# The last chunk of a fused Fourier mixing and feed-forward kernel: product order, sums read from PSUM, three queues for its stores

## The chip, the core and the metric

The kernel runs on one NeuronCore of a Trainium2 chip. A core has five engines with instruction streams of their own: TensorE (PE, matrix products), VectorE (DVE, elementwise), ScalarE (ACT, one-input functions and copies with a scale), GpSimd (POOL, elementwise in software) and SyncE (SP, which mainly issues transfers). They meet at semaphores. Transfers between on-chip memory (SBUF) and device memory are issued from the queues of SP, ACT or POOL and are carried out by the core's DMA engines. Products land in PSUM, from which ACT and DVE can read.

The metric is the device time of one execution in microseconds (us), lower is better.

## The reference

```python
def _attn_ref(x):                       # x: (8, 3008, 256), float32
    X = np.fft.fft(x, axis=1)
    X = np.fft.fft(X, axis=2)
    return X.real.astype(np.float32)

def _moe_ref(x, w_in, w_out):           # x: the result above as (24064, 256)
    h = x @ w_in                        # w_in: (256, 2048)
    relu6 = np.clip(h + 3.0, 0.0, 6.0)
    g = h * relu6 / 6.0
    return (g @ w_out).astype(np.float32)   # w_out: (2048, 256)
```

The real part of a two-dimensional Fourier transform of each of 8 sequences, then a feed-forward layer with the hard-swish function.

## The kernel before

The sequence axis of 3008 = 47 × 64 is transformed in two stages of matrix products (`stage1`, `stage2`). The transform along the 256 features is folded into the first weight matrix. The 8 sequences are worked in 4 pairs. Each pair's frequencies are cut into chunks of up to 256 columns, and a chunk holds frequencies together with their mirror images, so that one pass through `w_in` serves both: `mlp1` makes two products u and v, and u + v and u − v are the hidden values of a frequency and of its mirror.

A chunk takes 8 steps (`fc` = 0 to 7), each of which handles two blocks of 128 hidden units. The order of the work is written out by hand: a loop over all steps of all chunks calls `mlp1` two steps ahead, `combine` one step ahead, and `mlp2` for the step itself, with the transform stages of the next pair and the finishing of the previous chunk put between at fixed steps.

The second product (`mlp2`) uses a scheme of Strassen's kind: seven products of 128x128 weight blocks in place of eight. Their moving operands are three of the activated blocks, `a`, and four sums of them, `c`, which `combine` makes in three additions, one after another (the last of them is the operand of product 6). The seven products accumulate over the 8 steps in four PSUM tiles, `ch.acc[0]` to `ch.acc[3]`: products 0 and 1 in the first, 2 and 3 in the second, 4 and 5 in the third, 6 in the fourth. Product 3's operand is the first of the `c`.

At a chunk's last step ACT copies the tiles to an SBUF tile `e`, scaled by 1 / WS (line 472). The four output blocks are then sums of products: with P0 to P6 for the scaled products, in `r[m, h]`, where `m` is the frequency or its mirror and `h` a half of the features,

- r[0, 0] = P0 + P1
- r[0, 1] = P0 − P5 + P3 + P6
- r[1, 0] = P0 − P5 + P4 + P2
- r[1, 1] = P0 − P5 + P4 + P3

For all chunks but the last, `finish` makes these on GpSimd in the background. Each block is then turned in 32x32 squares by VectorE (`turn`, line 522) into a tile `o`, and each `o` leaves in stores of 32 KB (`send`, line 528), each with 4 x 32 runs of 256 B.

For the very last chunk (`ch.final`, 192 columns) nothing is left to hide behind, and it has a path of its own. `combine` of its last step runs on VectorE. ACT evacuates only the first two PSUM tiles. `finish_final` makes the sums on VectorE, reading products 4 to 6 straight from PSUM through `add_product` (line 498), turns each block as soon as it is made, and sends the first `o` (m = 0, 6 stores) before it makes the second (m = 1, 6 stores). The stores alternate between the queues of SP and ACT.

After the last instruction come the closing waits and a barrier of all engines, which the profile books under the line of the program's launch, L1001 before the change and L1008 after it. Every engine goes through a DRAIN there before the barrier. SP waits for the semaphores of all transfers.

Of the kernel before, what the change touches and what calls it, by code (L numbers as in the profile page):

```python
# [48 lines left out]
WS = 2.0 ** 20  # L49
# [9 lines left out]
def kernel(  # L59
# [10 lines left out]
    nc = tc.nc  # L70
# [4 lines left out]
    NF = NFC // 2  # L75
# [35 lines left out]
    out_k = out.rearrange("(p bj i k1) (q e) -> p k1 bj q i e", p=NP, k1=N1, i=DH, e=2 * DH)  # L111
# [325 lines left out]
    def add(out, in0, in1, eng=None):  # L437
        (eng or nc.gpsimd).tensor_tensor(out, in0, in1, op=AL.add)  # L438
# [17 lines left out]
    def mlp2(ch, fc):  # L456
        a = ch.a.pop(fc)[:].rearrange("p m f n -> p (m f) n")[:, :, 0:ch.n]
        c = ch.c.pop(fc)
        moving = [a[:, 0], a[:, 1], a[:, 3], c[:, 0], c[:, 1], c[:, 2], c[:, 3]]
        for i, mv in enumerate(moving):  # L460

            if fc == 0 and i % 2 == 0:
                ch.acc[i // 2] = ps_a.tile([P, 2, TB], F32, tag="acc", name="acc")
            nc.tensor.matmul(ch.acc[i // 2][:, i % 2, 0:ch.n], G[:, i, fc, :], mv,  # L464
                             start=(fc == 0 and i % 2 == 0), stop=(fc == NF - 1), skip_group_check=True)
            if fc == NF - 1 and (i % 2 == 1 or i == 6):
                if i == 1:
                    ch.e = epool.tile([P, 8, TB], F32, tag="e", name="e")
                k = 2 * (i // 2)
                if ch.final and k >= 4:  # L470
                    continue
                nc.scalar.mul(ch.e[:, k:i + 1, 0:ch.n], ch.acc[i // 2][:, 0:i + 1 - k, 0:ch.n], 1.0 / WS)  # L472

# [14 lines left out]

    def finish_final(ch):
        n = ch.n  # L490
        e = ch.e[:, :, 0:n]
        w = epool.tile([P, 3, TB], F32, tag="w", bufs=1, name="w")
        ch.r = epool.tile([P, 2, 2, TB], F32, tag="r", name="r")
        wn, rn = w[:, :, 0:n], ch.r[:, :, :, 0:n]
        os = [epool.tile([P, TB // DH, 2, DH], F32, tag="o", name="o") for m in range(2)]

        def add_product(out, i, in1, sign=1.0):
            nc.vector.scalar_tensor_tensor(out, ch.acc[i // 2][:, i % 2, 0:n], sign / WS, in1,
                                           op0=AL.mult, op1=AL.add)

        add(rn[:, 0, 0], e[:, 0], e[:, 1], nc.vector)
        turn(ch, os[0], 0, 0)
        add_product(wn[:, 0], 5, e[:, 0], -1.0)
        add(wn[:, 2], wn[:, 0], e[:, 3], nc.vector)
        add_product(rn[:, 0, 1], 6, wn[:, 2])
        turn(ch, os[0], 0, 1)
        send(ch, os[0], 0)
        add_product(wn[:, 1], 4, wn[:, 0])
        for h in range(2):
            add(rn[:, 1, h], wn[:, 1], e[:, 2 + h], nc.vector)  # L510
            turn(ch, os[1], 1, h)
        send(ch, os[1], 1)

    def store(ch, m):
        o = epool.tile([P, TB // DH, 2, DH], F32, tag="o", name="o")
        for h in range(2):
            turn(ch, o, m, h)
        send(ch, o, m)

    def turn(ch, o, m, h):  # L520
        n = ch.n
        nc.vector.transpose(o[:, 0:n // DH, h], ch.r[:, m, h, 0:n].rearrange("p (j i) -> p j i", i=DH))  # L522

    def send(ch, o, m):

        queues = [nc.sync, nc.scalar] if ch.final else [nc.sync]
        for j, (bj, k1) in enumerate(ch.blocks[m]):
            queues[j % len(queues)].dma_start(out=out_k[ch.pr.p, k1, bj], in_=o[:, j].rearrange("p h e -> p (h e)"))

    pairs = [Pair(p) for p in range(NP)]  # L530
    first = pairs[0]
# [347 lines left out]
    for s, (p, ck, fc) in enumerate(steps):  # L879
# [24 lines left out]
        else:  # L904
# [8 lines left out]
            if prev and fc < 3:  # L913
                if fc > 0:
                    store(prev, fc - 1)
                elif not prev.first:
                    finish(prev)
            mlp2(*chunk(s))
        if fc == NF - 1:
            prev = chunks[p][ck]  # L920
    finish_final(prev)


# [82 lines left out]
```

## Time and profile before

| | |
|---|---|
| median of 3 runs | 1947.92 us (1947.09 to 1950.45) |
| span of the profiled execution | 1945.0 us |
| TensorE matmul busy | 1927.7 us, 99% of the span |
| VectorE / GpSimd / ScalarE busy | 1437.7 / 1416.1 / 682.5 us |
| granted TensorE clock, mean | 0.998 |
| DMA, mean over the span | 50 GB/s |

The page gives the busy time of each engine, the chain of waits that ended last, the groups of instructions by line, and the transfers. The chain is TensorE's for 94% of the span. The change, however, concerns only what comes at the very end. There the last product begins at 1935.10 us, the last instruction of VectorE at 1938.16 us, and the span ends at 1945.03 us. The queries that matter are therefore the timeline and the table of stretches for the last 15 us, and the instructions of the closing block. The busy time of an engine says nothing here, since from 1935.4 us on no engine has much to do.

### The profile page before, as it was taken

Reading aid. Unit: us, or ns where it says so; the run is one execution under the profiler, and the core shown is the slowest. Engines: PE = TensorE matmul, PEld = TensorE weight load, DVE = VectorE, ACT = ScalarE, POOL = GpSimd, SP = SyncE. Lnnn points to the kernel's source line nnn. Section 1 sums busy time; section 2 is a strip of 40 time slices with the busy share of each in tenths; the row PEclk is TensorE's granted clock in tenths of the full one; section 3 lists DMA queues with packets and bytes.
Section 4 is the critical chain, followed back from the end, with each engine's and each line's share of the span. In section 5 each row is a group of like instructions: output and inputs, shape, how many; then the busy total and the mean of one; then the engine's idle time right before and its main releaser. Section 6 shows DMA issues by size and latency. Waiting matters only on the chain.

```text
span 1945.0 us, 27925 instructions
## 1 busy us (share of the span) xinstructions
PE 1927.7 (99%) x9254; PEld 1658.3 (85%) x9254; DVE 1437.7 (74%) x2777; ACT 682.5 (35%) x1167; POOL 1416.1 (73%) x1620
## 2 busy tenths in 40 slices
PE   9999999999999999999999999999999999999997
PEld 4678888888998888888898888888899888888887
DVE  6877777777777777777787777777778777777777
ACT  5633333333333333333333333333333333333332
POOL 4078888877688887787678887878666667666664
PEclk9999999999999999999999999999999999999999
DMA  8531312211112132111111221212110101101000
GB/s 235 170 80 40 81 48 57 55 44 31 39 28 55 49 81 57 44 50 31 38 36 45 57 55 44 49 52 52 35 28 20 28 17 27 35 12 28 20 19 20
DMA packets 148959, 96.71 MB, mean 50 GB/s; under 512 B 117791, under 2 KB 131235, under 8 KB 148814
## 3 DMA queue, kind: packets, MB, share of 16 engines
q1 hardware_dynamic: 137350, 58.06, 12.5%
q0 software_dynamic: 10672, 36.67, 6.7%
q8 instruction: 73, 1.20, 0.3%
q14 instruction: 72, 0.59, 0.1%
q10 hardware_dynamic: 792, 0.20, 0.0%
HBM read 57.57 MB, written 37.32 MB: 49 GB/s over the span
## 4 chain that ended last, share of the span: by engine, by line
PE 94%; DVE 3%; ACT 1%; DMA 1%; issue 0%; SPq 0%; DVEq 0%; POOL 0%; ACTq 0%
PE acc L464 56%; PE v L379 16%; PE u L379 16%; PE ps L328 2%; PE ps L223 1%; DVE a L424 1%; PE acc L448 1%; DMA xt<-in_x_dram,IX 1%; DVE s L384 1%; ACT t L421 1%; PE spare L635 0%; DVE o L522 0%; DVE u L405 0%; ACT PM L574 0%; PE ps L278 0%
## 5 line engine op out<-in xcount | busy, mean ns | idle before, releaser
L438 POOL TENSOR_TENSOR c<-a 128x512 f32<-128x512 f32 (+1 forms) x375 | 469.5, 1252 | 363.5 <-PE acc L464 317.5
L464 PE MATMUL acc<-c,G 128*128 128x256 f32 (+1 forms) x3008 | 696.9, 374 | 0.0
L421 ACT ACTIVATE t<-u,half 128x512 f32<-128x512 f32 (+1 forms) x384 | 260.7, 679 | 1143.7 <-DVE u L394 1064.7
L464 PEld LDWEIGHTS acc<-c,G 128*128 128x128 f32 x3008 | 565.4, 190 | 71.1
L384 DVE SCALAR_TENSOR_TENSOR s<-qn,WN,u 128x256 f32<-128x256 f32 (+1 forms) x768 | 330.1, 471 | 333.4 <-PE u L379 332.6
L464 PE MATMUL acc<-a,G 128*128 128x256 f32 (+1 forms) x2256 | 541.2, 375 | 0.0
L464 PEld LDWEIGHTS acc<-a,G 128*128 128x128 f32 x2256 | 421.3, 189 | 71.2 <-issue 17.5
L379 PE MATMUL v<-q,W 127*128 127x256 f32 (+1 forms) x1536 | 389.0, 375 | 2.3 <-DVE a L424 2.3
L379 PE MATMUL u<-q,W 128*128 128x256 f32 (+1 forms) x1536 | 388.0, 375 | 0.0
L424 DVE SCALAR_TENSOR_TENSOR a<-t,u 128x512 f32<-128x512 f32 (+2 forms) x448 | 263.7, 600 | 103.4 <-ACT t L421 99.6
L379 PEld LDWEIGHTS v<-q,W 127*128 127x128 f32 x1536 | 288.3, 190 | 42.1 <-DVE a L424 1.9
L379 PEld LDWEIGHTS u<-q,W 128*128 128x128 f32 x1536 | 285.7, 190 | 35.2 <-issue 0.5
L438 POOL TENSOR_TENSOR c<-a,c 128x256 f32<-128x256 f32 (+1 forms) x375 | 269.0, 717 | 29.4
L438 POOL TENSOR_TENSOR c<-c,a 128x256 f32<-128x256 f32 (+1 forms) x375 | 268.8, 717 | 29.4
L394 DVE TENSOR_TENSOR u<-s,v 128x512 f32<-128x512 f32 x352 | 245.0, 696 | 38.1 <-DVE s L384 1.8
L424 DVE SCALAR_TENSOR_TENSOR a<-t,v 128x512 f32<-128x512 f32 (+1 forms) x480 | 263.4, 565 | 0.2
L421 ACT ACTIVATE t<-v,half 128x512 f32<-128x512 f32 (+1 forms) x384 | 260.6, 679 | 0.5 <-PE acc L464 0.4
L396 DVE TENSOR_TENSOR v<-v,s 128x512 f32<-128x512 f32 x352 | 243.7, 692 | 0.0
L438 POOL TENSOR_TENSOR r<-w,e 128x256 f32<-128x256 f32 (+1 forms) x92 | 88.8, 987 | 3.6
L472 ACT ACTIVATE e<-acc 128x512 f32<-128x512 f32 (+2 forms) x186 | 84.4, 544 | 3.4 <-PE acc L464 3.3
L522 DVE STREAM_TRANSPOSE o<-r 128x256 f32<-128x256 f32 (+1 forms) x192 | 72.5, 415 | 0.2
L438 POOL TENSOR_TENSOR w<-w,e 128x512 f32<-128x512 f32 (+1 forms) x46 | 57.6, 1252 | 3.6
(104 smaller groups left out, 778.0 us busy)
## 6 DMA issues: line engine op xcount, KB each, us to landing
out_dram<-o SPq DMA_DIRECT2D x746, 32.0 KB
zd<-z SPq DMA_DIRECT2D x48, 192.0 KB
g<-zd SPq DMA_DIRECT2D x36, 256.0 KB
xt<-in_x_dram POOLq DMA_DIRECT2D x21, 256.0 KB, 3.7
qn<-qd SPq DMA_DIRECT2D x19, 256.0 KB
st<-in_moe_w_in_dram POOLq DMA_DIRECT2D x8, 512.0 KB, 7.6
st<-in_moe_w_out_dram POOLq DMA_DIRECT2D x8, 512.0 KB, 5.6
xt<-in_x_dram POOLq DMA_DIRECT2D x17, 192.0 KB, 4.0
```

Of the source, the lines that this page charges most:

```text
L223: nc.tensor.matmul(ps[b][h * PB:(h + 1) * PB, 0:n], F[rows(b), 0:PB], y[rows(b), 2 * h:2 * h + n], start=True, stop=not last, skip_group_c ...
L328: nc.tensor.matmul(ps[:, blk, u * P:n].rearrange("p (b k) -> p b k", b=2), g[:, kk, blk * (P + 1):blk * (P + 1) + P], T[:, :, gr, blk, kk, ...
L379: nc.tensor.matmul(ps[:, i, 0:nq], W1[r, blk, f * P:(f + 1) * P], q[r, blk, of:of + nq], start=True, stop=True)
L384: nc.vector.scalar_tensor_tensor(s[:, i, 0:nq], qn[:, of:of + nq], WN[:, f:f + 1], u[:, i, 0:nq], op0=AL.mult, op1=AL.add)
L394: nc.vector.tensor_tensor(u[:], s[:], v[:], op=AL.add)
L396: nc.vector.tensor_tensor(v[:], v[:], s[:], op=AL.subtract)
L421: nc.scalar.activation(t, h, AF.Relu, bias=half[:], scale=scale)
L424: nc.vector.scalar_tensor_tensor(dst, t, 1.0, h, op0=AL.min, op1=AL.mult)
L438: (eng or nc.gpsimd).tensor_tensor(out, in0, in1, op=AL.add)
L464: nc.tensor.matmul(ch.acc[i // 2][:, i % 2, 0:ch.n], G[:, i, fc, :], mv, start=(fc == 0 and i % 2 == 0), stop=(fc == NF - 1), skip_group_c ...
L472: nc.scalar.mul(ch.e[:, k:i + 1, 0:ch.n], ch.acc[i // 2][:, 0:i + 1 - k, 0:ch.n], 1.0 / WS)
L522: nc.vector.transpose(o[:, 0:n // DH, h], ch.r[:, m, h, 0:n].rearrange("p (j i) -> p j i", i=DH))
```

## The change

The edits touch the last chunk alone.

1. In its last step the products are made in the order 0, 1, 2, 3, 4, 6, 5: product 5, which three of the four output blocks need, comes last in place of product 6, which one needs.
2. ACT evacuates only product 0 (128x192), the one that is added to everything. All others are read from PSUM by VectorE where they are needed. The purpose is a shorter evacuation ahead of the first sum.
3. The sums are put in another order: those that don't need product 5 first. The second half, m = 1, has one more VectorE instruction than before, since P0 − P5 is no longer shared between the halves.
4. The stores leave by three queues: SP, ACT, POOL, SP, ACT, and the sixth by POOL for m = 0 and by SP for m = 1. The purpose is to spend less time on issuing.

```diff
@@ mlp2
-        for i, mv in enumerate(moving):
+        order = list(enumerate(moving))
+        if ch.final and fc == NF - 1:
+            order[5:] = order[:4:-1]
+        for i, mv in order:
...
-                if ch.final and k >= 4:
+                if ch.final:
+                    if k == 0:
+                        nc.scalar.mul(ch.e[:, 0, 0:ch.n], ch.acc[0][:, 0, 0:ch.n], 1.0 / WS)
                     continue
@@ finish_final
-        e = ch.e[:, :, 0:n]
+        e = ch.e[:, 0, 0:n]
...
-        add(rn[:, 0, 0], e[:, 0], e[:, 1], nc.vector)
+        add_product(rn[:, 0, 0], 1, e)
         turn(ch, os[0], 0, 0)
-        add_product(wn[:, 0], 5, e[:, 0], -1.0)
-        add(wn[:, 2], wn[:, 0], e[:, 3], nc.vector)
-        add_product(rn[:, 0, 1], 6, wn[:, 2])
+        add_product(wn[:, 0], 3, e)
+        add_product(wn[:, 2], 6, wn[:, 0])
+        add_product(rn[:, 0, 1], 5, wn[:, 2], -1.0)
         turn(ch, os[0], 0, 1)
         send(ch, os[0], 0)
-        add_product(wn[:, 1], 4, wn[:, 0])
+        add_product(wn[:, 1], 4, e)
+        add_product(wn[:, 0], 5, wn[:, 1], -1.0)
         for h in range(2):
-            add(rn[:, 1, h], wn[:, 1], e[:, 2 + h], nc.vector)
+            add_product(rn[:, 1, h], 2 + h, wn[:, 0])
             turn(ch, os[1], 1, h)
@@ send
-        queues = [nc.sync, nc.scalar] if ch.final else [nc.sync]
+        queues = [nc.sync, nc.scalar, nc.gpsimd, nc.sync, nc.scalar, (nc.gpsimd, nc.sync)[m]]
         for j, (bj, k1) in enumerate(ch.blocks[m]):
-            queues[j % len(queues)].dma_start(out=out_k[ch.pr.p, k1, bj], in_=o[:, j].rearrange("p h e -> p (h e)"))
+            (queues[j] if ch.final else nc.sync).dma_start(out=out_k[ch.pr.p, k1, bj], in_=o[:, j].rearrange("p h e -> p (h e)"))
```

The order of the products among the instructions of TensorE, and the waits of all other chunks, stay as they were: with the last chunk left aside, the two programs have the same instructions in the same order on every engine.

## The prediction

> **What bounds the kernel now.** I read the page first, then the last 15 us of the timeline, then the DMA share of the same stretch, then the instructions of the closing block. The page says that the body is TensorE's and that only its ends are open:
>
> ```profile
> PE 1927.7 (99%) x9254; PEld 1658.3 (85%) x9254; DVE 1437.7 (74%) x2777; ACT 682.5 (35%) x1167; POOL 1416.1 (73%) x1620
> ...
> PE 94%; DVE 3%; ACT 1%; DMA 1%; issue 0%; SPq 0%; DVEq 0%; POOL 0%; ACTq 0%
> ```
>
> The edits are all in the final chunk's last step, so nothing before about 1933 us can move. The timeline from there (start, length, engine, line, operation):
>
> ```profile
> 1933.89 1.08 ACT L472 ACTIVATE e<-acc 128x384 f32<-128x384 f32 x2 [3.35 <-PE acc L464]
> 1933.96 1.46 PE L464 MATMUL acc<-c,G 128*128 128x192 f32 x8
> 1934.42 0.36 DVE L438 TENSOR_TENSOR r<-e 128x192 f32<-128x192 f32 x1 [1.45 <-ACT e L472]
> 1934.82 0.38 DVE L522 STREAM_TRANSPOSE o<-r 128x192 f32<-128x192 f32 x1
> 1935.13 0.36 DVE L498 SCALAR_TENSOR_TENSOR w<-acc,e 128x192 f32<-128x192 f32 x1
> 1935.60 0.36 DVE L438 TENSOR_TENSOR w<-w,e 128x192 f32<-128x192 f32 x1
> 1936.06 0.36 DVE L498 SCALAR_TENSOR_TENSOR r<-acc,w 128x192 f32<-128x192 f32 x1
> 1936.45 0.38 DVE L522 STREAM_TRANSPOSE o<-r 128x192 f32<-128x192 f32 x1
> 1936.76 0.32 DVE L498 SCALAR_TENSOR_TENSOR w<-acc,w 128x192 f32<-128x192 f32 x1
> 1936.86 3.77 SPq L528 DMA_DIRECT2D out_dram<-o  x6
> 1936.86 4.87 ACTq L528 DMA_DIRECT2D out_dram<-o  x6
> ...
> 1938.16 0.38 DVE L522 STREAM_TRANSPOSE o<-r 128x192 f32<-128x192 f32 x1
> ```
>
> TensorE ends at 1935.42, VectorE at 1938.54, the issuing of stores at 1941.73 (ACT's queue), the span at 1945.03. What happens in the last 8 us is transfer:
>
> ```profile
> 1938.00:1938.50 0.50, 0.00 (x0) 0.00 (x0) 0.47 (x2) 0.00 (x0) 0.00 (x0) 0.57 0.27 61
> 1938.50:1943.50 5.00, 0.00 (x0) 0.00 (x0) 0.04 (x1) 0.00 (x0) 0.00 (x0) 0.50 0.32 72
> 1943.50:1944.00 0.50, 0.00 (x0) 0.00 (x0) 0.00 (x0) 0.00 (x0) 0.00 (x0) 0.50 0.04 8
> ```
>
> The last two columns are DMA share and GB/s: flat at 0.32 and 72 for five microseconds without a gap. The trace's packets are as flat, 144 in every half microsecond. So the 12 stores (132 packets each, 1584 in all, 5.5 us at 288 a us) are limited by their transfer, not by when VectorE hands them over: the first packet is at 1938.04, 1.18 us after the first issue, the last ends at 1943.60, its semaphore lands at 1943.93, and 1.10 us of closing waits and barrier follow. That chain sets the end now. Beside it GpSimd, idle since 1930.56, goes through its closing block:
>
> ```profile
> L1001 POOLq DRAIN  x1: 9788/9788/9788, 1929.9 to 1929.9; - x1
> ```
>
> It starts at 1929.93 and ends at 1939.72, 9.16 us after the engine's last addition. Nobody feels it, since the last store lands 4 us later.
>
> **What the Trainium skill says.** "DMA: Bandwidth & Descriptors", section "Why a DMA increments its semaphore by 16 and not by 1": a transfer uses the largest number of DMA engines, up to 16, that divides both sides' slowest dimension, and on the hardware path the lowest-numbered ones. The store's DRAM side begins with a dimension of 4. The trace agrees: each store's semaphore is raised five times, once by the sequencer and four times from the engines, and four engines at 72 packets a us each make the 288. The same page, "Issuing engines are not separate DMA queues": more issuing engines save only issue time. The trace agrees for SP and ACT, whose packets share one flat rate; for GpSimd's software path the first section says that the engines are taken from a moving start, so its stores need not share those four; no store here shows it. "Perfetto Trace Analysis", "DMA Instruction — HWDGE": the issue's length includes a wait for a lock on the one descriptor generator; the trace has 0.54 us for SP's issue alone and up to 1.38 for ACT's first. "PSUM — Partial Sum Buffer", "Engine vs sequencer instructions": a drain waits for its engine to go fully idle. Here GpSimd's drain lasts 9.16 us longer than its last instruction, so more than that is in it; no page prices it.
>
> **The change, part by part.**
>
> 1. Products 5 and 6 change places on TensorE: the same matmuls; product 6 needs the last combined operand, written by 1932.97, and would start at 1934.61. Nothing.
> 2. ACT evacuates one 192-column block in place of two of 384. It still starts at 1933.89, because its wait is for product 1. The page has 353 ns for 128x192 and 491 for 128x384: VectorE starts 0.14 us earlier, at 1934.28. The second evacuation was hidden and goes unnoticed.
> 3. VectorE's chain. Steps from start to start, from the timeline: addition to transpose 0.40, transpose to an independent instruction 0.30, a dependent one behind two waits 0.46, to a transpose behind one 0.39. Up to the first send both versions have six instructions and the same waits, so the second transpose starts at 1936.30 and the first send is at 1936.71, 0.15 earlier. After it there are six instructions in place of five: w = P4 + e, then w − P5, new. I take PSUM reads at the old prices, since L498 reads PSUM and takes 320 to 358 ns against 315 to 359 for L438's additions. 1936.60, 1936.96, 1937.35, 1937.75, 1938.05, 1938.42: the last transpose starts 0.26 later, and the second send is at about 1938.83.
> 4. The queues: SP 2 + 3 stores, ACT 2 + 2, GpSimd 2 + 1. If GpSimd's stores run on other DMA engines, the four have 9 stores: 4 from the first send, done by about 1939.75, then 5 × 0.458 = 2.29 us from 1938.83 + 1.18 = 1940.01, so the last packet is at 1942.30 in place of 1943.60. GpSimd's last store is issued at 1938.83 (0.53 to 0.58 us by L165 and L555) and lands by 1941.5 to 1942.7, with the 2.7 to 3.9 us from issue to landing of its loads: hidden. By itself this part is worth **−1.3 us**.
> 5. The wait that it adds. GpSimd now has three stores ahead of its drain, the first waiting for VectorE until 1936.71, the last until 1938.83. Behind the last stands only the drain, and behind that the barrier on which all engines wait. The drain can start at about 1939.4. If its 9.16 us are its own cost, it ends at 1948.56; the barrier took 0.75 us from GpSimd's release (1944.28 to 1945.03), so the span ends at 1949.3, **+4.3 us**. The bounds of this cost: 0.05 to 0.1 us (the drain at the program's start, which follows only memsets, and the two later ones of the closing block) and 9.16. I take 9.16: all engines but GpSimd were at work in that time, none of their events coincides with 1939.72, and the cheap drains are those with no transfer or arithmetic issued since the drain before.
>
> **Rivals.**
>
> - **A, the drain's time recurs:** 1947.92 + 4.3 = 1952.2. For: the 9.16 us are in the trace, with GpSimd idle, and lie inside GpSimd. Against: one sample, and GpSimd's spans are rough; if its end is misdated, nothing is there.
> - **B, no drain, transfers relieved:** 1947.92 − 1.3 = 1946.6. For: the transfer limit is plain and a quarter of it is moved away. Against: it needs A's drain to be an artefact or to depend on something that doesn't recur.
> - **C, no drain, and GpSimd's stores on the same four engines:** then 12 stores again, 1937.89 + 5.5 = 1943.4 for the last packet, 0.2 earlier than now: 1947.7.
> - **D, the drain's clock starts only when GpSimd's last store has landed** (1941.5 to 1942.7): ends near 1951.3, plus 0.75: 1952 in the span, +7, 1955.
>
> **How the numbers follow.** A 0.56, B 0.26, C 0.10, D 0.05, something upstream 0.03. The forecast is A's, 1952.2. The range takes in A to C: 1945.9 (B less the 0.7 us by which its latencies could be off) to 1953.2 (A with a drain up to 1 us longer), and leaves D out. The three runs before lie between 1947.09 and 1950.45, so a microsecond of scatter is in it too. The bound of 0.2% is 3.9 us: A lies 0.4 above it, so I count 0.36 of its 0.56 as slower and 0.20 as same; D is slower; B and C are same; of the rest 0.02 is faster and 0.01 slower. Faster 0.02, same 0.56, slower 0.42. Most of "same" is not no effect.
>
> **What would show it.** Right, if the closing block shows a GpSimd drain of about 9 us that begins near 1939.4 and ends last, with the last store landed 6 us before it. Wrong, if that drain is short: then B's signs would be a last packet near 1942.3 and the span near 1943.7; C's, packets at 288 a us for 5.5 us. For step 2, VectorE's first instruction of the finish starts 0.14 earlier; for step 3, the first send is 0.15 earlier and the last transpose 0.26 later than now. A first send that is not earlier, or PSUM reads well over 0.36 us, would break step 3. A second drain cost, or a start of the drain at the landing, would put the time at D.

## The result and the profile after

The changed kernel takes 1953.15 us (median of 6 runs, 1952.52 to 1956.85) against 1948.49 us of the kernel before, run beside it (6 runs, 1946.97 to 1950.45). The ratio of all runs is 1.0028, 95% interval 1.0015 to 1.0041: slower by 0.28% (the medians alone, 4.66 us apart, give 0.24%).

The page of the changed kernel, busy time by engine and then the chain by engine:

```profile
PE 1930.7 (99%) x9254; PEld 1659.4 (85%) x9254; DVE 1438.5 (74%) x2778; ACT 682.0 (35%) x1166; POOL 1418.4 (73%) x1623
...
PE 93%; DVE 3%; DMA 1%; ACT 1%; issue 1%; SPq 0%; POOL 0%; DVEq 0%; POOLq 0%; ACTq 0%
```

The body does the same work. The new name in the chain is POOLq, GpSimd's instruction queue, with a share that rounds to nothing: the cost lies in the last 16 us of 1954. The timeline there (start, length, engine, line, operation):

```profile
1938.80 0.33 ACT L476 ACTIVATE e<-acc 128x192 f32<-128x192 f32 x1 [3.34 <-PE acc L468]
1938.86 1.46 PE L468 MATMUL acc<-c,G 128*128 128x192 f32 x8
1939.16 0.36 DVE L504 SCALAR_TENSOR_TENSOR r<-acc,e 128x192 f32<-128x192 f32 x1 [1.28 <-ACT e L476]
...
1941.55 3.85 SPq L535 DMA_DIRECT2D out_dram<-o  x5
1941.55 3.48 ACTq L535 DMA_DIRECT2D out_dram<-o  x4
1941.80 0.36 DVE L504 SCALAR_TENSOR_TENSOR w<-acc,w 128x192 f32<-128x192 f32 x1
1941.82 1.53 POOL L535 DMA_DIRECT2D out_dram<-o  x2 [6.35 <-DVE w L504]
1942.19 0.36 DVE L504 SCALAR_TENSOR_TENSOR r<-acc,w 128x192 f32<-128x192 f32 x1
...
1943.24 0.38 DVE L529 STREAM_TRANSPOSE o<-r 128x192 f32<-128x192 f32 x1
1943.92 0.69 POOL L535 DMA_DIRECT2D out_dram<-o  x1 [0.56 <-DVE o L529]
```

This execution reached its last chunk 4.9 us later than the one shown of before (runs differ by that much). To compare tails, all times below that are called "on the tail's clock" count from the start of ACT's first evacuation in the finish, 1933.89 before and 1938.80 after. The line of the launch, L1008, within the last 15 us (durations in ns, smallest, median, largest):

```profile
L1008 POOLq DRAIN  x1: 10098/10098/10098, 1943.9 to 1943.9; - x1
```

The drain begins while GpSimd still has its last store to issue. That issue ends at 1944.61 and the drain at 1953.99, 9.387 us later. Every transfer has landed by 1949.15. From 1949.6 on, when SP has gone through its last waits, nothing runs but GpSimd's drain, and 0.79 us after it the span ends. Before, the same drain ended 4.2 us ahead of the last landing.

The transfers, by stretch (last two columns: DMA share, GB/s):

```profile
1942.50:1944.50 2.00, 0.00 (x0) 0.00 (x0) 1.04 (x4) 0.00 (x0) 1.43 (x3) 0.88 0.34 64
1944.50:1946.50 2.00, 0.00 (x0) 0.00 (x0) 0.00 (x0) 0.00 (x0) 0.11 (x1) 0.50 0.44 75
1946.50:1948.50 2.00, 0.00 (x0) 0.00 (x0) 0.00 (x0) 0.00 (x0) 0.00 (x0) 0.50 0.27 59
```

Not flat any more, and not faster: the share rises to 0.44 where before it was 0.32, but the bytes move at 59 to 75 GB/s against 72. The last landing (the moment when a store's semaphore is complete) is at 10.36 us on the tail's clock, where before it was at 10.03: the third queue did not even bring the output home sooner.

The tails, in us on the tail's clock:

| kernel | first send | last landing | GpSimd's closing drain ends | span ends |
|---|---|---|---|---|
| before | 2.96 | 10.03 | 5.82 | 11.13 |
| changed | 2.75 | 10.36 | 15.20 | 15.99 |
| e1, sums alone | 2.75 | 9.82 | 5.83 | 10.92 |
| e2, queues alone | 2.97 | 10.48 | 15.02 | 15.80 |
| e3, late copy | 2.97 | 10.04 | 13.79 | 14.59 |
| e4, two early drains | 2.75 | 10.46 | 8.67 | 11.99 |
| e5, nine stores | 2.75 | 8.74 | 5.83 | 9.96 |
| e7, three early drains | 2.75 | 10.01 | 8.25 | 11.54 |
| e8, eight stores cut by rows | 2.75 | 8.26 | 5.83 | 9.30 |
| e9, changed, 162 transfers | 2.75 | 9.99 | 9.78 | 11.22 |
| e10, all stores cut by rows | 2.75 | 7.85 | 5.82 | 9.20 |

### The profile page after: what moved, and what is told of

It reads as the page before. It is cut to its first block, busy times and chain, and to the rows that moved or that the text cites. A ratio compares the mean times of both kernels' runs of the same rounds, so it can differ in the third digit from the quotient of the medians.

```text
span 1954.8 us, 27925 instructions
## 1 busy us (share of the span) xinstructions
PE 1930.7 (99%) x9254; PEld 1659.4 (85%) x9254; DVE 1438.5 (74%) x2778; ACT 682.0 (35%) x1166; POOL 1418.4 (73%) x1623
## 4 chain that ended last, share of the span: by engine, by line
PE 93%; DVE 3%; DMA 1%; ACT 1%; issue 1%; SPq 0%; POOL 0%; DVEq 0%; POOLq 0%; ACTq 0%
PE acc L468 56%; PE v L379 16%; PE u L379 16%; PE ps L328 2%; PE ps L223 1%; DVE a L424 1%; PE acc L448 1%; DMA xt<-in_x_dram,IX 1%; DVE s L384 1%; ACT t L421 1%; PE ps L278 0%; PE spare L642 0%; DVE u L405 0%; DVE o L529 0%; DMA T<-in_c_stage_dram 0%
```

## The experiments

**Which edit costs it.** e1 is the changed kernel without the third queue, e2 the kernel before with it.

```diff
-        queues = [nc.sync, nc.scalar, nc.gpsimd, nc.sync, nc.scalar, (nc.gpsimd, nc.sync)[m]]
+        queues = [nc.sync, nc.scalar] * 3
```

> The changed kernel with the twelve stores dealt to SP and ACT in turn, as before: the product order and the sums from PSUM alone. Theory (all of the loss is GpSimd's drain): the drain falls back to where nobody feels it, the first send is 0.15 to 0.2 us earlier, the twelve stores need 5.5 us from there as they did, so the span is 0.2 us shorter than before's, time ratio 0.9999 (0.998 to 1.001). Rival (the longer chain behind the first send, or PSUM reads, cost something): 0.3 us or more longer than before, with a gap in the packets between the two sends.

```diff
-        queues = [nc.sync, nc.scalar] if ch.final else [nc.sync]
+        queues = [nc.sync, nc.scalar, nc.gpsimd, nc.sync, nc.scalar, (nc.gpsimd, nc.sync)[m]]
...
```

> The kernel before with the three-queue send alone. Theory: GpSimd's last store is issued at the second send as in the changed kernel, so its drain ends about 9.4 us after it and the span is 4.4 to 4.9 us longer than before, ratio 1.0024. Rival (the sums add to the loss): 1 us or more less than that.

e1: ratio to before 0.9998 (0.9990 to 1.0007), and a tail 0.21 us shorter, as the first send is 0.21 earlier. e2: 1.0024 (1.0015 to 1.0032), a tail 4.67 us longer. GpSimd's drain in e2:

```profile
L1001 POOLq DRAIN  x1: 10095/10095/10095, 1939.5 to 1939.5; - x1
```

It ends 9.386 us after the issue of GpSimd's last store. The queues carry the loss; the other edits by themselves gain 0.2 us. Beside the third queue they gain nothing: the changed kernel's tail is 0.18 us longer than e2's, since its last transpose, for which GpSimd's last store waits, comes 0.18 us later (4.45 against 4.27).

**Is it the late transfer or any late instruction?** e3 keeps all stores on SP and ACT and gives GpSimd a copy at the end.

```diff
         send(ch, os[1], 1)
+        late = epool.tile([P, TB], F32, tag="late", bufs=1, name="late")
+        nc.gpsimd.tensor_copy(late[:, 0:n], ch.r[:, 1, 1, 0:n])
```

> The kernel before, all stores on SP and ACT, with one GpSimd copy of 128x192 added that waits for VectorE's last addition and moves nothing through DMA. Theory (the closing drain has a cost of its own that begins when GpSimd's last instruction ends): the copy ends near 1938.7 on before's clock, the drain 9.16 us later, the span is 3.6 us longer, ratio 1.0018. Rival (the drain waits for something of the late transfers, or the late stores are what makes it long): the drain ends where it did or within 1 us of the copy, and the span is before's within 0.3 us.

The ratio is 1.0018 (1.0011 to 1.0025). The timeline of e3, then the line of its launch:

```profile
1939.51 0.34 POOL L514 COPY late<-r 128x192 f32<-128x192 f32 x1 [7.63 <-DVE r L438]
```

```profile
L1003 POOLq DRAIN  x1: 9523/9523/9523, 1939.5 to 1939.5; - x1
```

The copy ends at 1939.85, the drain at 1949.01, 9.159 us later, to the nanosecond what it was before. The tail is 3.46 us longer. So the drain pays its own price from the end of GpSimd's last instruction, whatever that is. The stores on SP and ACT ran at 144 to 146 packets in each half microsecond beside this drain, as before, and landed at 10.04 against 10.03, so the drain doesn't slow them.

**What does the price depend on?** Before issued 111 software transfers (transfers from GpSimd), the changed kernel 114, and 9.159 and 9.387 us differ by 76 ns for each of the three. e4 and e7 put further drains into GpSimd's stream: e4 one right behind loads that had just been issued and one 189 us after the last (first diff), e7 three, at 8.8 us or more behind the last load (second diff).

```diff
+    DRAINS = ((1, 0, 0), (NP - 1, 1, 0))
...
+        if (p, ck, fc) in DRAINS:
+            nc.gpsimd.drain()
```

```diff
+        if (ck, fc) == (0, 2) and p > 0:
+            nc.gpsimd.drain()
```

> The changed kernel with two more GpSimd drains: one at the start of the second pair of images, when 62 software transfers have been issued, one in the second chunk of the last pair, when 49 more have. Theory (a drain pays about 82 ns for each software transfer issued since the drain before): they last 5.1 and 4.0 us beyond the work ahead of them, and the closing one, with three stores since, under 0.5 us; then the stores set the end, 0.3 us later than before's, plus what the two stalls cost TensorE (0 to 8 us, to be read at its last product). Rival one (a fixed cost of a drain): about 9.2, 9.2 and 9.4 us. Rival two (a price for all transfers ever issued): 5.1, 9.2 and 9.4. Rival three (the closing drain alone is long): under 0.3 us for the two new ones, 9.4 for the last.

> The changed kernel with three more GpSimd drains, each some 10 us after the last transfer was issued: early in the second pair (62 software transfers since the start), in the third (26 more) and in the fourth (23 more). Theory (82 ns for each transfer, and where one is still under way the drain also waits for it): 5.1, 2.2 and 2.0 us beyond the work ahead of them, and the closing one ends 0.2 us after GpSimd's last store has landed, 2.9 us after its issue. Rival (the first transfers cost more than the later ones, as the 6.4 us of the earlier run for 62 suggests): 6.4 us again for the first, 2.2 and 2.0 for the others.

e4's drains lasted 6.37 and 4.09 us beyond the work ahead of them, and the closing one 2.86. The totals of both kernels hold the stalls of the drains added (e4 1.0031, 1.0020 to 1.0042; e7 1.0010, 1.0001 to 1.0018), so the tails are what to read. In e7, GpSimd's timeline ahead of the first drain, and the three drains:

```profile
557.30 0.72 POOL L438 TENSOR_TENSOR c<-a,c 128x256 f32<-128x256 f32 x1
```

```profile
L892 POOLq DRAIN  x1: 5918/5918/5918, 557.3 to 557.3; - x1
L892 POOLq DRAIN  x1: 2974/2974/2974, 1026.8 to 1026.8; - x1
L892 POOLq DRAIN  x1: 2720/2720/2720, 1494.0 to 1494.0; - x1
```

Each was fetched while the addition ahead of it ran. The first ends at 563.18, 5.16 us after that addition; the others, read alike, last 2.21 and 1.96 us. For 62, 26 and 23 transfers that is what 82 ns for each gives. With these already paid, the closing drain no longer holds the end. It isn't the half microsecond expected of e4, since it waits for transfers under way: in e7 it ends 0.16 us after GpSimd's last store has landed (1943.91), in e4 too (1948.55), and SP's stores set the end. What 6.37 us for 62 transfers in e4 has above 5.1 stays open. Transfers were under way then, but so were GpSimd's stores in the changed kernel and in e2, where nothing was added.

**By transfer or by byte?** e6, e11 and e12 cut direct loads of the kernel before into two by rows: more transfers, the same bytes. The diff is e6's; in e11 it is done where pr.p == 1, in e12 where pr.p > 1.

```diff
-            nc.gpsimd.dma_start(out=o[:, 0:n, :], in_=rows[:, c * XC + 1:c * XC + 1 + n, :])
+            for r in (slice(0, 32), slice(32, nr)):
+                nc.gpsimd.dma_start(out=o[r, 0:n, :], in_=rows[r, c * XC + 1:c * XC + 1 + n, :])
```

> The kernel before with each of the 48 direct x loads of pairs 1 to 3 cut into two by rows: 48 more software transfers, 159 in place of 111, with the same bytes and the same rows. Theory (the drain pays about 82 ns for each transfer issued since the drain before): it ends 13.1 us after GpSimd's last addition in place of 9.16, still just hidden behind the stores, and the time is before's within 0.2%. Rivals (a fixed cost, or a cost by bytes or packets): 9.2 us.

> The kernel before with the direct x loads of the second pair alone cut into two by rows: 127 software transfers. If what is done is cleared at the 128th, none has been cleared and the drain lasts 127 x 82 + 71 ns = 10.5 us beyond GpSimd's last addition; if it is cleared at the 122nd, 0.5 to 0.6 us. It is hidden either way: time as before.

> The kernel before with the direct x loads of the third and fourth pair cut into two by rows: 143 software transfers. With a clearing at the 128th that leaves the last few standing, as 159 transfers and 3.2 us suggest, 143 - 121 = 22 are left and the drain lasts 1.9 us; with a price that keeps growing, 11.8 us. Hidden either way: time as before.

The tails are before's (11.13 to 11.14 us), and the ratio of e6 is 0.9997 (0.9989 to 1.0006); e11 and e12 ran once each and have none. e6's drain was not as expected: with 159 transfers it lasted 3.20 us, neither 13.1 nor 9.2. In GpSimd's stream one gap is new, 0.46 us right behind the 128th transfer, where neighbours of its kind follow each other without one. The line of e6's launch:

```profile
L1002 POOLq DRAIN  x1: 3822/3822/3822, 1931.5 to 1931.5; - x1
```

That suggested that transfers are cleared there, and 38 (3.2 us) of the 159 left. e11 and e12 were made for it. With 127 transfers the drain lasted 10.47 us (10.5 expected); with 143, GpSimd's timeline and the line of the launch of e12:

```profile
1929.83 0.59 POOL L439 TENSOR_TENSOR c<-a,c 128x192 f32<-128x192 f32 x1
```

```profile
L1002 POOLq DRAIN  x1: 2517/2517/2517, 1929.8 to 1929.8; - x1
```

1932.31 less 1930.42 is 1.89 us, with a gap of 0.44 us behind the 128th again. All drains with nothing under way, by transfers issued since the one before:

```
transfers        23     26     49     62     111    127    | 143        159
us measured      1.957  2.206  4.085  5.156  9.159  10.465 | 1.891      3.198
76 + 81.8 ns x n 1.957  2.203  4.084  5.148  9.156  10.465 | n-121: 1.876  3.184
```

The line is drawn through the first and the sixth. Six kernels with 111 transfers gave 9.158 to 9.160 us. From 49 to 62 transfers the bytes grow by 67% and the drain by 26%, as the count does, and the sixth moves the bytes of the fifth. The price goes by transfer. Why 121 are left out behind the 128th stays open. It isn't the number of those that were done: none of GpSimd's packets ran in the 37 us ahead of the 128th transfer's in e6, and in the 39 us ahead of the 127th's in e12, so 127 and 126 were through.

**The change without its drain.** e9 is the changed kernel with e6's cut, so that the 128th transfer comes early.

> The changed kernel with the 48 direct x loads of pairs 1 to 3 cut into two by rows, so that 162 software transfers are issued in all. In the kernel before the same cut left a drain of 3.2 us in place of 9.2, as if only those from about the 122nd on were still to be paid. Theory (at 128 entries GpSimd clears what is done, and the closing drain pays 82 ns for each of the about 41 transfers since): it ends 3.4 us after GpSimd's last store is issued, within 0.3 us of the last landing, and the span ends 11.9 to 12.2 us after ACT's evacuation starts, 4 us less than with the change (16.0) and 0.8 to 1.1 more than before (11.1): ratio to before 1.0005. Rival (the short drain of that run had to do with the idle time behind the last transfer): about 13.4 us, and a span of 20 us.

Ratio 1.0002 (0.9994 to 1.0010). Its drain:

```profile
L1009 POOLq DRAIN  x1: 4688/4688/4688, 1938.9 to 1938.9; - x1
```

It lasted 3.98 us from the end of the last issue, 0.6 more than expected, which stays open, and ended ahead of SP's last wait. The loss of the change is gone, with its three queues and sums kept. So is any gain: the end is at 11.22 us on the tail's clock (11.9 to 12.2 were expected), before's at 11.13 and e1's at 10.92.

**Why do nine stores take as long as twelve?** e5 leaves GpSimd's three stores out, so three blocks of the output are not written.

```diff
+            if not ch.final or queues[j] is not nc.gpsimd:
...
```

> The changed kernel without GpSimd's three stores: three of the last twelve 32 KB blocks are not written, the nine others leave by SP and ACT as in the changed kernel. Theory (GpSimd's packets held up the other nine): four stores from the first send are through before the second, the five others run at 288 packets a us, the last lands 8.3 us after ACT's evacuation starts (before 9.6, with the change 10.4) and the span ends at 9.5 to 9.7 us, 1.3 to 1.5 us less than before. Rival (the four DMA engines, or the issuing on SP and ACT, are slow for another reason): the last landing stays above 9.3 us. GpSimd's drain is hidden in both.

The last landing is at 8.74, the end at 9.96, the ratio 0.9994 (0.9986 to 1.0003). The stretches of e5:

```profile
1942.50:1943.50 1.00, 0.00 (x0) 0.00 (x0) 0.00 (x0) 0.00 (x0) 0.00 (x0) 0.50 0.23 51
1943.50:1945.50 2.00, 0.00 (x0) 0.00 (x0) 0.00 (x0) 0.00 (x0) 0.00 (x0) 0.50 0.32 72
```

A dip between the two sends, as the prediction had it, then the old flat 72 GB/s. With GpSimd's stores in, the last of the same nine landed 1.25 to 1.72 us later (9.99 to 10.46 in the four kernels with these sums), although SP and ACT issued them at the same times (the last issue ended at 6.60 in both). The packets show the collision as it happens. In the changed kernel GpSimd's first store ran from 4.90 to 5.52 on the tail's clock, and between 5.0 and 5.5 SP and ACT began 23 packets where e5 began 126. Its second ran from 5.68 to 6.48, and between 6.0 and 6.5 they began 26 where e5 began 116. The Trainium skill ("DMA: Bandwidth & Descriptors", section "SWDGE vs HWDGE vs iDMA") says that each DMA engine has 16 queues, of which software and hardware transfers feed different ones, and goes through them in turn. The trace agrees as far as it shows: GpSimd's data went in packets of 4096 bytes that took 0.20 us at the median, SP's and ACT's in packets of 256 bytes at 18 ns, and the four raisings of a store's semaphore from its engines, within 0.03 to 0.06 us before, spread over up to 1.1 us. That the stores hold each other up is shown; that they do so by turns on the same engines is not, since which engines GpSimd's packets ran on isn't recorded. (The "9.6" and "9.4" for landings of before and of e1 in two expectations leave out the last store; the table has 10.03 and 9.82, and the 8.3 expected of e5 is as much too low. The "7.7" for e8 in e10's is 8.26 likewise.)

**A version that beats both.** If four DMA engines limit the tail, more engines should shorten it. e8 and e10 keep the sums, use SP and ACT alone, and cut stores by rows so that both sides' slowest dimension is 32, which by the section quoted in the prediction means 16 DMA engines. The diff is the core of e10's; e8 leaves blocks 4 and 5 of each send as they were.

```diff
...
+                for q in range(4):
+                    (nc.sync, nc.scalar)[q % 2].dma_start(
+                        out=out_k[ch.pr.p, k1, bjs, q].rearrange("b i e -> i b e"),
+                        in_=o[q * DH:(q + 1) * DH, js].rearrange("p j h e -> p j (h e)"))
...
```

> The changed kernel's sums with stores on SP and ACT alone, and eight of the twelve cut otherwise: blocks 0 to 3 of each send go as four transfers of 32 rows by four blocks, so that the slowest dimension is 32 on both sides in place of 4; blocks 4 and 5 as they were; SP issues seven, ACT five. Theory (the four DMA engines are the limit of the last 6 us): the eight spread over 16 engines, more than 288 packets a us run, the last landing comes at 8.6 us after ACT's evacuation starts (9.4 with the sums alone, 9.6 before), the span ends at 10.2, 0.9 us less than before. Rival (issuing the twelve is as slow as transferring them): 9.2 to 9.4 us and no gain.

> The changed kernel's sums with all stores of the last chunk on SP and ACT and cut by 32 rows: eight transfers a send, four of 32 rows by four blocks and four of 32 rows by two. The run with eight of twelve cut so ended 9.3 us after ACT's evacuation started (11.1 before), and its last landing, at 7.7, was of a store still on four DMA engines, as was ACT's one long issue of 1.3 us. If that store sets the end, the last landing is now 7.2 to 7.6 and the end 8.8 to 9.2 us; if issuing 16 transfers takes more than it saves, the end is 9.3 us or later. Ratio to before 0.9990 (0.998 to 1).

e8: ratio 0.9992 (0.9983 to 1.0000), end at 9.30. e10: 0.9992 (0.9983 to 1.0000), end at 9.20, 1.9 us less than before (0.2 of them the sums'). The timeline of e10, then its stretches:

```profile
1936.90 3.85 SPq L538 DMA_DIRECT2D out_dram<-o  x8
1936.90 3.93 ACTq L538 DMA_DIRECT2D out_dram<-o  x8
```

```profile
1938.00:1938.50 0.50, 0.00 (x0) 0.00 (x0) 0.50 (x2) 0.00 (x0) 0.00 (x0) 1.00 0.63 142
...
1939.50:1940.00 0.50, 0.00 (x0) 0.00 (x0) 0.00 (x0) 0.00 (x0) 0.00 (x0) 0.50 0.21 50
1940.00:1940.50 0.50, 0.00 (x0) 0.00 (x0) 0.00 (x0) 0.00 (x0) 0.00 (x0) 0.50 0.61 139
1940.50:1941.00 0.50, 0.00 (x0) 0.00 (x0) 0.00 (x0) 0.00 (x0) 0.00 (x0) 0.50 0.61 134
```

142 GB/s where twelve stores never got above 72, and each store now raises its semaphore 16 times from the engines in place of 4, as the section says. There is a dip between the sends, and the last store lands 1.60 us after its issue begins, ACT's first 1.71 us after (2.89 for before's last). So transfers no longer queue up; they wait for VectorE and for the issuing. e8 did better than expected. e10's end only just reached the slow end of what was expected of it, and its landing, at 7.85, missed 7.2 to 7.6. Sixteen issues took no longer than twelve had (3.9 us a queue). The gain shows plainly in the tail; in the whole time it is 0.1%, at the edge of its interval.

## Why the prediction was right or wrong

- **Steps 1 and 2 held.** VectorE started 0.36 us after ACT, predicted 0.39, before 0.52.
- **Step 3 held.** On the tail's clock the first send came at 2.75 (predicted 2.82, before 2.96), the last transpose at 4.45 (4.53; 4.27), the second send at 4.86 (4.94; 4.81). Reading PSUM cost nothing extra: 320 to 359 ns a sum.
- **Step 4 failed.** Its -1.3 us supposed that GpSimd's stores leave the other nine alone. That sum was good for nine stores by themselves: its last packet at 1942.30 plus the 0.33 us to the landing is 8.74, which is e5's to the hundredth, in part by luck (the second send came 0.08 us sooner than reckoned, and the rest took 0.08 longer). Beside GpSimd's stores the landing came at 10.36, 0.33 later than before. Rival C's sum was the nearer one: twelve stores in one line, with the last packet at 1943.4, which is 9.51 on the tail's clock. The last packet ended at 9.51 in e9, 9.55 in e7, 9.87 in the changed kernel and 9.96 in e4, as if GpSimd's stores had used the same four engines. It changed nothing in the forecast, which A's drain set, but rival B was built on it: e4, e7 and e9, with the drain out of the way, ended 0.1 to 0.9 us later than before, not 1.3 earlier.
- **Step 5 held as a mechanism and was 0.57 us short.** +4.28 was worked out, +4.85 came in the tail. Two terms: GpSimd's last store ended its issue at 5.81 on the tail's clock rather than 5.51 (it started 0.27 us after SP's of the same send, and took 0.69 us), and the drain lasted 9.387 us rather than 9.16, since the three stores added to what it pays for. The barrier made up the other 0.04. The Trainium skill ("VectorE: DVE Perf Modes", section "The DRAIN you can't avoid") puts the drains of a program's start and end at about 12 ns on every engine; SP's 7 ns are near that, GpSimd's 9.16 us are not, and the measurement decides.
- **The step that failed the forecast was how the chances were laid.** The time, 1952.2, was within 1 us of what came, 0.57 us of it because before itself ran at 1948.49 rather than 1947.92; the top of the range, 1953.2, was just above it. But B and C, in which no drain recurs, were given 0.36 because the drain had been seen once and might be an artefact; it is none (e3 repeats its 9.159 us to the nanosecond, at another time, behind a copy); and 0.20 of A's 0.56 was called "same", since A lay only 0.4 us above the bound of 3.9. So "same" was held likeliest, and the answer was slower, by 4.66 us in the medians. What the trace held against B was read but not weighed enough: 9.16 us of an engine that did nothing else, with no event of another engine at its end. And the three things that could be mis-sized in A, the issue, the transfers added, the barrier, all pushed upwards. Rival D, a drain that starts at the landing, is excluded: GpSimd's last store landed at 8.42 on the tail's clock, and the drain was over at 15.20, 6.8 us later and 9.39 after the issue's end.

## What to carry to other kernels

Before giving an engine a last instruction, look at what stands behind it in its closing block: in these runs GpSimd's drain cost some 82 ns for each transfer issued since the drain before it (up to 127 of them), and it is hidden only where GpSimd is done well before the others. If a kernel's tail is made of stores, look first at how many DMA engines each uses (here a slowest dimension of 4 against 32: 72 against up to 142 GB/s), and only then at more queues. When a forecast lies near the line between two answers, ask which way each unpriced term can push it.

## What the runs showed of the hardware that was not expected

- GpSimd's drain takes 76 ns and 81.8 ns for each software transfer issued since the drain before it, by transfer and not by byte, from 23 to 127 transfers with none under way; a copy as GpSimd's last instruction delays it just as a store does.
- At the 128th transfer the stream pauses for 0.44 to 0.46 us, and the drain then lasts as if only those beyond the 121st counted (1.89 us for 143, 3.20 us for 159).
- Three 32 KB stores of GpSimd beside nine of SP and ACT delayed the last of the nine by 1.25 to 1.72 us.
- The issue of a store of 32 rows took 0.32 to 0.45 us on SP and ACT in e10; one of 4 x 32 runs takes 0.54 to 0.70, and ACT's first 1.38.
